# A state-space convolution and a feature-map attention on one core: the written order, read-out engines, PSUM rings, per-unit forms and warm-up products set anew

## The chip, the core and the metric

The kernel runs on one core of one Trainium2 chip. The metric is the device time of one execution in microseconds (us). A core has five engines that matter here: PE (TensorE, with its weight loads shown apart as PEld), DVE (VectorE), ACT (ScalarE), POOL (GpSimd) and SP (the engine whose queue issues most of the DMAs). Each works through its own list of instructions in order; semaphores hold an instruction back until what it reads is there.

## The reference

Two branches of the same input `x` (2048 rows of 512 channels) are mixed by a gate. Branch `a` is a long convolution: a kernel K of 2048 taps per channel is a sum over 128 complex exponentials, and the convolution is done with FFTs. Branch `b` is linear attention of 32 heads of width 16 whose feature map is a softmax of +p and of -p.

```python
g = sigmoid((x * gate_w).sum(-1, keepdims=True))
P = exp(logdA[:, :, None] * l[None, None, :])            # logdA = exp(log_dt) * (A_re + i A_im)
K = einsum("dn,dnl,dn->dl", Cc, P, dB).real
a = irfft(rfft(pad(x)) * rfft(pad(K)))[:2048] + x * Dskip
q, k, v = split_heads(x @ wqkv)
phi = lambda p: concat([softmax(p), softmax(-p)])        # p = q @ w_phi, k @ w_phi
kv, z = einsum(phi_k, v), phi_k.sum(over the rows)
b = (phi_q @ kv / (phi_q @ z + 1e-6)) @ wo
out = g * a + (1 - g) * b
```

## The kernel before, in words

The work is written as 1035 steps (`Plan.add`, `Plan.dma`), each with an engine, a name, what it depends on, and the buffers it takes and frees. They are made in five parts, and nothing in this making sets the order in which they are issued. `Plan.run` reads that order from a table, `ORDER`: two characters are the number of one step. Four more tables are read beside it. `SIDES` gives, for each step that can run on either of two engines (read-outs of PSUM, mostly ACT or DVE), which one. `RINGS` gives, for each step that can take its PSUM tile from either of two rings, which one. `FOURS` (one digit per unit) and `ZPS` (one per pair of key blocks) choose between two forms of a step. `WARM` gives a number to each step that writes a PSUM tile; `heat` (L1561) issues that many products of the identity with a finished table into the fresh tile before the real products, which then overwrite them. In the kernel before, `WARM` is "0".

The stages, by what ACT does, since its list falls into clear parts:

- **Start.** Loads of parameters, `u` (tile `UD`) and weights; sine tables `TB`, `TI`, `TJ` (L284 to L306); folding `w_phi` into the weights (`wtp`, `wps`); `x` transposed (`xps`); then for 16 row blocks keys, `pk` (L704), their exponentials `Ek`, the softmax sums `Zk` (L731, or by products `zk` L725 and L734 where `ZPS` is 1), their reciprocal by a logarithm and an exponential on ACT (`rz`, L741 to L743: `Zk` and the 17th plane of `vr`), values `vp` (L752), and `kn` (L769). In between, the FFT of `u` for each half: `psA` (L586), `psB` (L611), read out to `xst` and written to DRAM as `XUd`.
- **Tables of the exponentials.** `trg` (sines and cosines on ACT), from which DVE makes `Ctab` and `Dtab` (L378).
- **Four phases of four units.** A unit is 32 channels. For each phase ACT first makes eight `cs` tiles (sines, L68, from `args` L1019), then `E` (exponentials, from `args` L1041). DVE makes per unit `A` (L1102, L1107, and L1112 where `FOURS` is 0) and `R` (L1119, L1123); PE multiplies them, `kps` (L178); ACT reads it out to `KD`, PE makes `psA` (L185), ACT reads it to `XA`, and for each quarter of the channels PE makes `psB` (L191), ACT reads it to `XK`, DVE multiplies by `XUX`, PE makes `psz` (L1262), ACT reads it to `Zr`, and it goes through DRAM (`Zd`, `ZT`) to the products `psy` (L1360). The queries' attention (`pq`, `Eq`, `zs`, `den`, `apm`, `ax`, `ops`, `oT`) lies in between.
- **Tail.** The last units in smaller pieces, and the stores to `out` (L1384, L991), issued from SP or ACT.

ACT holds one set of function tables at a time. The steps `tabT` (the set with the sine) and `tabL` (the set with logarithm and exponential) load one by name (L65, `preload_act_table_set`); each is a step of its own, so its place is a place in `ORDER`. A step notes the set it wants (`tab="L"` or `"T"`), but `Plan.run` only asserts that the dependences in `deps` are kept, and `tab` is not one of them. Where an activation stands behind another set, the build puts an `ACT_TABLE_LOAD` ahead of it, with the line of the activation (L68); a logarithm and an exponential get a set each in that case.

## Time and profile before

| | |
|---|---|
| median of 3 runs | 258.6 us (257.18 to 258.92) |
| the profiled execution | 258.5 us; its span, first to last instruction, 256.7 us |
| mean granted TensorE clock | 0.934 |
| DMA | 34.85 MB, 136 GB/s over the span |
| `ACT_TABLE_LOAD` | 10 |

The page gives busy time by engine and, in 40 slices of the span (6.4 us each), the busy share in tenths, the granted TensorE clock and the DMA share. The stretches used below were asked of the trace with ACT's own events as borders: the start of the third table load at 72.15 us (sines for `trg`), the end of the fourth at 103.55, the starts of the fifth, seventh and ninth (127.19, 153.17, 193.31), the end of the read-outs `XA` of units 12 and 13 at 224.60, and the start of 9.9 us at the end in which ACT computes nothing more (246.80).

### The profile page before, as it was taken

Reading aid. Unit: us, or ns where it says so; the run is one execution under the profiler, and the core shown is the slowest. Engines: PE = TensorE matmul, PEld = TensorE weight load, DVE = VectorE, ACT = ScalarE, POOL = GpSimd, SP = SyncE. Lnnn points to the kernel's source line nnn. Section 1 sums busy time; section 2 is a strip of 40 time slices with the busy share of each in tenths; the row PEclk is TensorE's granted clock in tenths of the full one; section 3 lists DMA queues with packets and bytes.
Section 4 is the critical chain, followed back from the end, with each engine's and each line's share of the span. In section 5 each row is a group of like instructions: output and inputs, shape, how many; then the busy total and the mean of one; then the engine's idle time right before and its main releaser. Section 6 shows DMA issues by size and latency. Waiting matters only on the chain.

```text
span 256.7 us, 9697 instructions
## 1 busy us (share of the span) xinstructions
PE 203.7 (79%) x4302; PEld 140.2 (55%) x4322; DVE 232.7 (91%) x315; ACT 221.8 (86%) x307; POOL 7.9 (3%) x21
## 2 busy tenths in 40 slices
PE   0676999999964578898958676899998899896970
PEld 0565665755643424356646533775686566784540
DVE  7699989988799999999999998999999899987781
ACT  3989898999899999989999989999999999863640
POOL 5600000000000000000000000000000000000000
PEclk9999999999997579999999778999999999997995
DMA  6899000336510587300644079215775975991934
GB/s 204 163 219 216 1 3 4 108 111 175 156 33 0 182 241 216 107 4 23 187 128 124 12 212 249 87 44 125 247 167 156 243 194 95 230 336 62 214 72 82
DMA packets 52841, 34.85 MB, mean 136 GB/s; under 512 B 30528, under 2 KB 48320, under 8 KB 52800
## 3 DMA queue, kind: packets, MB, share of 16 engines
q1 hardware_dynamic: 51456, 33.78, 50.5%
q8 instruction: 33, 0.54, 1.0%
q10 hardware_dynamic: 1344, 0.46, 0.9%
q14 instruction: 8, 0.07, 0.1%
HBM read 21.38 MB, written 12.58 MB: 132 GB/s over the span
## 4 chain that ended last, share of the span: by engine, by line
PE 36%; DVE 23%; ACT 23%; DMA 7%; issue 7%; SPq 2%; POOL 0%; ACTq 0%; DVEq 0%; POOLq 0%
PE pk L704 6%; PE vp L752 5%; ACT cs L68 4%; PE kps L178 3%; DMA Zd<-Zr 2%; PE psz L1262 2%; ACT Zr L144 2%; DVE A L1102 2%; DMA ZT<-Zd 2%; ACT L65 2%; DVE R L1119 2%; ACT XA L144 2%; ACT XK L144 2%; DMA ax<-apd 2%; DVE A L1107 2%
## 5 line engine op out<-in xcount | busy, mean ns | idle before, releaser
L68 ACT ACTIVATE cs<-args 128x1024 bf16<-128x1024 f32 x32 | 31.1, 1061 | 0.4 <-PE args L1019 0.4
L178 PE MATMUL kps<-R,A 128*32 128x64 bf16 x1536 | 28.6, 230 | 3.0 <-issue 1.6
L178 PEld LDWEIGHTS <-A 128*32 128x32 bf16 x1536 | 26.5, 160 | 7.5 <-issue 4.4
L1102 DVE TENSOR_TENSOR A<-Ctab,Dtab 128x2048 bf16<-128x2048 bf16 x16 | 19.5, 1217 | 1.3 <-PE kps L178 1.3
L1123 DVE TENSOR_TENSOR R<-E,cs 128x2048 bf16<-128x2048 bf16 x16 | 19.5, 1216 | 0.1
L1107 DVE TENSOR_TENSOR A<-Ctab,Dtab 128x2048 bf16<-128x2048 bf16 x16 | 19.5, 1216 | 0.0
L1119 DVE TENSOR_TENSOR R<-E,cs 128x2048 bf16<-128x2048 bf16 x16 | 19.5, 1216 | 0.0
L144 ACT CAST Zr<-psz 128x1024 bf16<-128x1024 f32 (+1 forms) x17 | 16.5, 990 | 2.2 <-PE psz L1262 0.9
L68 ACT ACTIVATE Ek<-pk 128x512 bf16<-128x512 f32 x32 | 16.7, 600 | 1.8 <-PE pk L704 1.6
L68 ACT ACTIVATE Eq<-pq 128x512 bf16<-128x512 f32 (+1 forms) x28 | 16.7, 686 | 0.6 <-PE pq L838 0.5
L1233 DVE TENSOR_TENSOR t<-XUX,XK 128x2048 bf16<-128x2048 bf16 x14 | 16.9, 1215 | 0.4 <-ACT XK L144 0.4
L68 ACT ACTIVATE E<-args 128x1024 bf16<-128x1024 f32 x16 | 16.7, 1043 | 0.5 <-DVE R L1123 0.5
L611 PE MATMUL psB<-XAu,TB 64*128 64x128 bf16 x256 | 11.8, 250 | 6.6 <-ACT xst L144 3.4
L752 PE MATMUL vp<-WW,xT 128*128 128x512 bf16 x59 | 16.1, 404 | 0.5 <-issue 0.3
L144 ACT CAST XK<-psB 128x1024 bf16<-128x1024 f32 (+1 forms) x17 | 16.4, 992 | 0.0
L144 ACT CAST XA<-psA 128x1024 bf16<-128x1024 f32 (+1 forms) x16 | 15.8, 1017 | 0.6 <-PE psA L185 0.6
L838 PE MATMUL pq<-xT,Wqp 128*128 128x512 bf16 x64 | 15.6, 380 | 0.0
L704 PE MATMUL pk<-WW,xT 128*128 128x512 bf16 x58 | 15.0, 380 | 0.4 <-issue 0.2
L611 PEld LDWEIGHTS <-TB 64*128 64x128 bf16 x256 | 9.7, 111 | 9.9 <-issue 9.8
L1262 PE MATMUL psz<-t,TI 128*128 128x512 bf16 x41 | 13.2, 423 | 1.1 <-ACT XK L144 0.6
L185 PE MATMUL psA<-W,KD 128*64 128x128 bf16 x256 | 9.8, 221 | 4.9 <-ACT cs L68 2.9
L65 ACT ACT_TABLE_LOAD x10 | 12.8, 1283 | 0.9 <-PEq L1615 0.7
(206 smaller groups left out, 496.0 us busy)
## 6 DMA issues: line engine op xcount, KB each, us to landing
XUX<-XUd SPq DMA_DIRECT2D x32, 256.0 KB, 3.7
XUd<-xst SPq DMA_DIRECT2D x8, 512.0 KB, 3.0
ax<-apd SPq DMA_DIRECT2D x16, 256.0 KB, 4.8
Zd<-Zr SPq DMA_DIRECT2D x24, 128.0 KB, 3.1
ZT<-Zd SPq DMA_DIRECT2D x6, 512.0 KB, 5.3
UD<-in_A_u_dram SPq DMA_DIRECT2D x16, 128.0 KB, 4.3
XUd<-xst SPq DMA_DIRECT2D x8, 256.0 KB, 3.9
wqk<-in_B_wqkv_dram SPq DMA_DIRECT2D x1, 1024.0 KB, 5.8
```

Of the source, the lines that this page charges most:

```text
L65: return self.nc.scalar.preload_act_table_set(name)
L68: return self.nc.scalar.activation(**kw)
L144: self.nc.scalar.copy(out=o, in_=i)
L178: nc.tensor.matmul(kps[32 * dj:32 * dj + 32, g4, e, :], lhsT=A[:, ka, :, :, d].rearrange("p a b -> p (a b)"), rhs=R[:, kr, d, :], start=(i ...
L611: nc.tensor.matmul(box.ps[:, c2, sl, :], lhsT=fc.TB[rows, b0:b0 + 2].rearrange("p a b -> p (a b)"), rhs=X.t[rows, k, r0 + sl].rearrange("p ...
L704: nc.tensor.matmul(box.ps[:], lhsT=xT[:, st, kt, :], rhs=g.WW[:, kt, :], start=(kt == 0), stop=(kt == 3))
L752: nc.tensor.matmul(box.ps[:], lhsT=xT[:, st, kt, :], rhs=g.WW[:, 4 + kt, :], start=(kt == 0), stop=(kt == 3))
L1102: nc.vector.tensor_tensor(out=c.A[:, 0:2].rearrange("p o a b c -> p (o a) b c"), in0=g.C[U // 8][:, 0:2, :, d0 % 256:d0 % 256 + 32].rearra ...
L1107: nc.vector.tensor_tensor(out=c.A[:, 2:4].rearrange("p o a b c -> p (o a) b c"), in0=g.C[U // 8][:, 1:3, :, d0 % 256:d0 % 256 + 32].rearra ...
L1119: nc.vector.tensor_tensor(out=c.R[:, :, :, 32:64], in0=t.E[:, 1].unsqueeze(1).to_broadcast([128, 2, 32, 32]), in1=t.cs[:], op=ALU.mult)
L1123: nc.vector.tensor_tensor(out=c.R[:, :, :, 0:32], in0=t.E[:, 0].unsqueeze(1).to_broadcast([128, 2, 32, 32]), in1=t.cs[:, ::-1, :, ::-1], o ...
L1262: nc.tensor.matmul(box.ps[:, hb, :], lhsT=fc.TI[:, k].rearrange("p h a t -> p (h a t)"), rhs=box.t[:, k, 512 * hb:512 * hb + 512], start=( ...
```

## The change

No step, tile, deps entry or shape is changed. The six tables are:

```diff
-    ORDER = ("0405060B0C0D0H0K0d0e0f0y0z0A0L0s0t0u0I0708090J0M0P0g0h0i000S110j0k0l0N0102030T0m0n0o0Q2P0a0b0c0p0q0r0_0W2R100U0O0V120Y2S"
...
+    ORDER = ("0H0I0J0B0C0D2P2R0M0L0K0_000P0Q100d0e0f0y0z0A0p0q0r0s0t0u0708090405060j0k0l0g0h0i0102030a0b0c0m0n0o2v2y2t2x2u0S0U0T0V0W112w2Q"
...
-    SIDES = ("01111101001010101100111011001001100101010000101110000000000001100001100111110100010001100000000000000000000000000000"
-             "0000000000000000000000000000100110000000000000001000010")
-    RINGS = ("001010111111010010100000000000000000000010100000000000001110010000100000001001001010101010100111111110001011000011100001"
-             "1111")
-    WARM = ("0")
-    FOURS = ("0111100101011000")
-    ZPS = ("01000111")
+    SIDES = ("10110101001010101100110111111010010101010010001110000100000010110100101101010100010001100000000000000000000000000000"
+             "0000011000000000000000000011001100000000000000000000010")
+    RINGS = ("00101011111000011010000000000000000000101010000000000000011001000010000000100101001110101010011111101000111100101010"
+             "00010011")
+    WARM = ("00000000600000000060000000005000010000300000000000000030001202000100230210100000000005011060520300000000000000000100"
+             "00000000001000000000003")
+    FOURS = ("0111110101011000")
+    ZPS = ("01000101")
```

What that comes to, step by step: 25 read-outs change their engine, 13 from ACT to DVE and 12 back (`vb` 4 each way, `XAu` 3 and 2, those to `xst` 2 and 1, `bsg` 2 and 1, the copies `UDp` 1 and 2, `bs3` 1 to DVE, `xT` and `XA` 1 each to ACT). `selE` goes from DVE to POOL, `Wphi` from POOL to DVE. Two stores move from SP's queue to ACT's and one from ACT's to SP's. Unit 5 gets the form with four products (no L1112, twice the `kps` products); key pair 6 gets the form without `zk`. Ten steps take their PSUM tile from the other ring. The numbers of `WARM` add up to 67 at 25 places; four of these places, with 15, are `zp` steps whose pair has `ZPS` 0, and these return before the tile is made. The built program has 52 such products at 21 places. It has 30 `ACT_TABLE_LOAD`s, 10 with L65 and 20 with L68.

The first place is ACT's list where `trg` begins. Before:

```order
L68 ACTIVATE Zk<-Zk 128x128
L68 ACTIVATE vr<-Zk 128x4x32
L65 ACT_TABLE_LOAD
L68 ACTIVATE trg<-pb_267 128x1024
L68 ACTIVATE trg<-pb_266 128x1024
L144 CAST XAu<-psA 128x256x4 x2
L68 ACTIVATE trg<-pb_266 128x1024
L402 ACTIVATE pb_267<-pb_266 128x1024
```

and now:

```order
L65 ACT_TABLE_LOAD
L68 ACTIVATE trg<-pb_297 128x1024
L68 ACT_TABLE_LOAD
L68 ACTIVATE Zk<-Zk 128x128
L68 ACT_TABLE_LOAD
L68 ACTIVATE vr<-Zk 128x4x32
L68 ACT_TABLE_LOAD
L68 ACTIVATE trg<-pb_298 128x1024
L144 CAST vb<-vp 128x512
L144 CAST XAu<-psA 128x256x4
```

The seventh reciprocal of the softmax sums (`Zk`, `vr`) now stands between two sine steps; the eighth does too, further down the list, with three loads of its own.

The second place is ACT's list at the first phase's `cs` tiles. Before:

```order
L144 CAST xst<-psB 128x2x4x4x32 x2
L68 ACTIVATE cs<-args 128x1024 x8
L65 ACT_TABLE_LOAD
L68 ACTIVATE E<-args 128x1024
L68 ACTIVATE Eq<-pq 128x4x128 x4
L68 ACTIVATE E<-args 128x1024
L68 ACTIVATE Eq<-pq 128x4x128 x8
```

and now:

```order
L144 CAST xst<-psB 128x2x4x4x32 x2
L68 ACT_TABLE_LOAD
L68 ACTIVATE E<-args 128x1024
L68 ACT_TABLE_LOAD
L68 ACTIVATE cs<-args 128x1024 x2
L68 ACT_TABLE_LOAD
L68 ACTIVATE Eq<-pq 128x4x128 x2
L68 ACT_TABLE_LOAD
L68 ACTIVATE cs<-args 128x1024 x6
L68 ACT_TABLE_LOAD
L68 ACTIVATE E<-args 128x1024
L68 ACTIVATE Eq<-pq 128x4x128 x2
```

One `E` and one pair of `Eq` have moved in ahead of and between the `cs` tiles; the `tabL` step itself (L65) comes nine activations behind the last row.

The third place is the end of ACT's list. Before:

```order
L144 CAST Zr<-psz 128x512 x2
L144 CAST Zr<-psz 128x1024
L991 DMA out_dram<-xT 32x4x384 x2
L1384 DMA out_dram<-xT 512x1x128 x2
```

and now:

```order
L1384 DMA out_dram<-xT 32x12x256 x2
L144 CAST xT<-bps 128x2x128
L144 CAST Zr<-psz 128x512 x2
L144 CAST Zr<-psz 128x1024
L65 ACT_TABLE_LOAD
L1384 DMA out_dram<-xT 512x1x128 x2
L1384 DMA out_dram<-xT 32x12x256 x2
```

Four stores of other quarters came to ACT and the two of L991 left it; two of the four now stand behind the store of the last quarter.

By the stretches named above, the table loads stand like this (from ACT's two lists; a stretch of the change is the one with the same activations):

| stretch of before, us | loads before | loads now |
|---|---|---|
| 0 to 72.15 | 2 | 2 |
| 72.15 to 103.55 | 2 | 12 |
| 103.55 to 127.19 | 0 | 1 |
| 127.19 to 153.17 | 2 | 7 |
| 153.17 to 193.31 | 2 | 5 |
| 193.31 to 224.60 | 2 | 2 |
| after 224.60 | 0 | 1 |

33 lines of the change are left out of this document (16 added, 17 removed).

## The prediction

> **What bounds the kernel now.** I read the page's busy times first, then a table of stretches cut at ACT's own events, then ACT's rows at a table load.
>
> ```profile
> PE 203.7 (79%) x4302; PEld 140.2 (55%) x4322; DVE 232.7 (91%) x315; ACT 221.8 (86%) x307; POOL 7.9 (3%) x21
> ...
> PE 36%; DVE 23%; ACT 23%; DMA 7%; issue 7%; SPq 2%; POOL 0%; ACTq 0%; DVEq 0%; POOLq 0%
> ```
>
> No engine owns the chain (the second row): it changes hands. The shares are means, so the stretches decide. Columns: from and to, length, then busy us of PE, PEld, DVE, ACT, POOL, then the granted clock, the DMA share and GB/s.
>
> ```profile
> 0.00:72.15 72.15, 57.90 (x911) 40.24 (x921) 62.55 (x110) 62.18 (x105) 7.91 (x21) 1.00 0.50 122
> 72.15:103.55 31.40, 20.60 (x307) 12.54 (x309) 30.26 (x51) 30.79 (x32) 0.00 (x0) 0.78 0.47 139
> 103.55:127.19 23.64, 20.84 (x515) 12.40 (x513) 23.43 (x35) 22.02 (x40) 0.00 (x0) 1.00 0.26 74
> 127.19:153.17 25.98, 18.81 (x462) 12.73 (x463) 25.91 (x29) 24.97 (x31) 0.00 (x0) 0.87 0.43 118
> 153.17:193.31 40.14, 36.25 (x841) 26.58 (x843) 39.19 (x42) 39.37 (x49) 0.00 (x0) 0.96 0.58 152
> 193.31:224.60 31.29, 27.78 (x686) 20.88 (x684) 30.38 (x30) 29.26 (x31) 0.00 (x0) 1.00 0.78 186
> 224.60:246.80 22.20, 19.55 (x465) 13.44 (x464) 17.62 (x21) 13.19 (x21) 0.00 (x0) 0.92 0.65 186
> 246.80:256.70 9.90, 1.92 (x132) 1.35 (x130) 3.38 (x4) 0.00 (x0) 0.00 (x0) 0.68 0.42 82
> ```
>
> From 72.15 to 224.60, 152.45 us, DVE is busy 149.2 and ACT 146.4 (sums of five rows). Two engines are full at once: work taken off one alone gains little, but work put on ACT has only 152.45 - 146.41 = 6.0 us of idle time to go into. I call this stretch the middle. PE is busy 124.3 of it. Before and behind the middle all engines have gaps.
>
> **The table loads.** The change turns ACT's 10 table loads into 30. What one takes:
>
> ```profile
> L65 ACT ACT_TABLE_LOAD x10 | 12.8, 1283 | 0.9 <-PEq L1615 0.7
> ```
> ```profile
> 71.83 0.31 ACT L68 ACTIVATE vr<-Zk 128x128 bf16<-128x128 f32 x1
> 72.15 1.28 ACT L65 ACT_TABLE_LOAD   x1
> 73.44 2.01 ACT L68 ACTIVATE trg<-pb 128x1024 bf16<-128x1024 f32 x2
> 75.36 1.00 ACT L144 CAST XAu<-psA 128x1024 bf16<-128x1024 f32 x1
> ```
>
> The load waits for nothing and starts 0.01 us behind the activation (71.83 + 0.31 = 72.14), the next one 0.01 behind the load. Two ordinary instructions overlap: the pair ends at 75.45 and the cast starts at 75.36, 0.09 earlier. An inserted load therefore costs 1.28 + 0.01 + 0.09 = 1.38 us of ACT's time. Twelve loads instead of 2 stand in the stretch from 72.15 on, 1 instead of 0, 7 instead of 2 and 5 instead of 2 in the next three, 2 and 2 in the fifth: 10 + 1 + 5 + 3 = 19 more in the middle, 19 x 1.38 = **26.2 us**. The twentieth stands behind ACT's last read-out:
>
> ```profile
> 245.77 1.03 ACT L144 CAST Zr<-psz 128x1024 bf16<-128x1024 f32 x1
> 250.49 0.69 DVE L1373 TENSOR_TENSOR xT<-psy,gT 128x512 bf16<-128x512 f32 x1 [0.97 <-PE psy L1360]
> 251.21 1.66 ACTq L1384 DMA_DIRECT2D out_dram<-xT  x2
> ```
>
> What follows it on ACT is the last store, and that waits for DVE's product, 4.4 us after the read-out (246.80 to 251.18): the load lies in that gap and costs nothing; without the gap, 1.28.
>
> The middle's other work on ACT grows too. Two reciprocals that before ended at 72.14 are now between sine steps, four activations by the rows:
>
> ```profile
> L68 ACT ACTIVATE Zk<-Zk 128x128 f32<-128x128 f32 x8 | 2.6, 326 | 0.7 <-DVE Zk L734 0.7
> L68 ACT ACTIVATE vr<-Zk 128x128 bf16<-128x128 f32 x8 | 2.5, 311 | 0.3
> L144 ACT CAST vb<-vp 128x512 bf16<-128x512 f32 x7 | 4.2, 595 | 1.2 <-PE vp L752 0.8 <-DVE vr L761 0.4
> ```
>
> 2 x (0.326 + 0.311) = 1.3 us; two `vb` read-outs come to ACT there (1.2), and an `xst` read-out left it (about 1.0, as the cast at 75.36): **+1.5 us**. So ACT's work in the middle is at least 146.4 + 26.2 + 1.5 = 174.1 us, DVE's 149.2 and a little: ACT alone sets the middle. Of ACT's 6.0 us idle some vanishes, because DVE and PE, which it waited for, now run ahead; but ACT's order was not drawn around these loads, and an `E` or `XK` that comes late holds DVE, whose answer ACT needs a few rows on. Bounds: none left (174.1) and twice as much (186.1). I take half, 3.0, nearer the low end since 96% of ACT's middle is already work (146.4 of 152.45): 177.1, against 152.45, **+24.7 us**.
>
> The Trainium skill (ScalarE: Activation LUTs, What ACT_TABLE_LOAD costs) gives a switch of sets as about 1283 ns of load and a drain of about 1380 ns, 2.66 us together. The load is the row's number; of the drain the rows at 72.15 show nothing. By it, 19 x 2.66 = 50.5 us, an estimate, would come on top, about 308 us.
>
> **The dummy products.** 52 are in the program. A stream of the same shape, warm and at a low clock:
>
> ```profile
> 33.02 1.89 PE L704 MATMUL pk<-WW,xT 128*128 128x512 bf16 x8
> 94.89 1.46 PE L752 MATMUL vp<-WW,xT 128*128 128x512 bf16 x3
> ```
> ```profile
> L704 PE MATMUL pk<-WW,xT 128*128 128x512 bf16 x58 | 15.0, 380 | 0.4 <-issue 0.2
> ```
>
> One takes 0.380, so the seven others in 1.89 us follow at 0.216 each; three in 1.46 are at most 0.49 each. So the 52 are 11 us of PE (52 x 0.216), at most 25. Nearly all stand in the middle, where PE has 152.45 - 124.28 = 28 us free now and some 25 more when ACT stretches it. What they could gain is a higher clock where it falls to 0.78 and 0.87; there ACT is busy 98% and 96%, PE waits for it, and faster products end no wait. Bounds: a gain of 1 us, and a loss of 3 where six of them stand ahead of a `psB` that ACT waits for (6 x 0.49 = 2.9). I take 0. The cover is the table loads themselves; without them PE's 28 us must do.
>
> **Per-unit forms and engines.**
>
> ```profile
> L1112 DVE TENSOR_TENSOR A<-A 128x2048 bf16<-128x2048 bf16 x8 | 9.8, 1219 | 0.1
> L731 DVE TENSOR_REDUCE Zk<-Ek 128x64 f32<-128x1024 bf16 x8 | 9.3, 1208 | 0.0
> L734 DVE TENSOR_REDUCE Zk<-zk 128x128 f32<-128x512 f32 x4 | 2.8, 692 | 1.4 <-PE zk L725 1.3
> ```
>
> Unit 5 loses one sum (-1.22), key pair 6 gets two long reductions for a short one (2 x 1.21 - 0.69 = +1.73), and the moved read-outs nearly cancel (13 against 12): DVE has about 1 us more. It is hidden by ACT's 25; if ACT were not late, it would cost its 1 us. The other PSUM rings and the products of unit 5 in place of `zk` likewise lie in PE's free time.
>
> **Start and tail.** At the start PE waits for the first weights, which now are first on SP's queue, 0.47 us sooner:
>
> ```profile
> 7.09 1.89 PE L525 MATMUL wtp<-ident,wqk 128*128 128x128 bf16 x16 [7.09 <-DMA wqk<-in_B_wqkv_dram]
> 1.20 0.42 SPq L1507 DMA_DIRECT2D wqk<-in_B_wqkv_dram  x1
> 0.73 0.40 SPq L211 DMA_DIRECT2D Bim<-in_A_B_im_dram  x1
> 8.42 1.05 POOL L468 TENSOR_TENSOR Wphi<-wc,mask 128x512 bf16<-128x512 bf16 x1 [4.50 <-DMA wc<-in_B_w_phi_dram]
> ```
>
> But `Wphi` is now on DVE ahead of the read-out of those products, and waits for a DMA that lands at 8.42; behind it `wT` and all that PE does next are queued. These two about cancel. ACT gets to its first sine step without the two reciprocals and without the last sums: 1.3 us less work in a stretch in which it is idle 10.0 us, so between 0 and 2: **-1.0**. At the end ACT issues four stores where it issued two (1.66), the added two by
>
> ```profile
> 251.21 1.34 SPq L1384 DMA_DIRECT2D out_dram<-xT  x2
> ```
>
> 1.34 us later than the last store before: +1.3. DVE, no longer the last to be late, may give back some of the 9.1 us from the end of the last `E` to the end of that unit's last sum:
>
> ```profile
> 221.71 1.05 ACT L68 ACTIVATE E<-args 128x1024 bf16<-128x1024 f32 x1
> 230.59 1.22 DVE L1112 TENSOR_TENSOR A<-A 128x2048 bf16<-128x2048 bf16 x1
> ```
>
> Of it six instructions of DVE, about 7 us, are that unit's own. Bounds -3 and +2 for the tail as a whole, I take **+1.0**.
>
> **The sum**, against the profiled execution's 258.5 us (span 256.7 and 1.8 around it; the median of the runs, 258.6, is the same within 0.1): 258.5 + 24.7 - 1.0 + 1.0 = 283.2, say **283 us**, slower by 9.5%. With the low ends (174.1 in the middle, -2, -1, -3) 274.2, with the high ends (186.1, +3, 0, +2) 297.2; high ends together are unlikely.
>
> **The rivals.**
>
> - *The loads go into idle time.* ACT's table loads wait for nothing, so they can run while ACT would wait for PE or DVE. For: a load needs no operand. Against: only 6.0 us idle in the middle. Were all of that used and the start and the tail 3 us and 5 us shorter through the new order, 258.5 + 21.7 - 8 = about 272. Below 273: 0.10.
> - *The order opens more waits than the loads.* With PE idle while ACT reloads, the clock falls to half over more of the middle, and the dummy products stand in front of real ones at that clock. For: the clock was 0.78 where PE was busy 20.60 of 31.40. Against: 96% of ACT's middle was work. Every term at its high end, 297. Above 293: 0.10.
> - *Each load drains the engine first.* The mechanism would be a wait of one long activation, some 1.04 us (E in the page's groups is below), at each of 19 loads: 283 + 20 = 303. Against: 0.01 us ahead of the load at 72.15. 0.02. The Trainium skill's rule above (ScalarE: Activation LUTs, What ACT_TABLE_LOAD costs) is of this kind.
>
> ```profile
> L68 ACT ACTIVATE E<-args 128x1024 bf16<-128x1024 f32 x16 | 16.7, 1043 | 0.5 <-DVE R L1123 0.5
> ```
>
> - *The loads do not run, the other side.* If the 20 loads of line 68 were merged away before they reach the chip, 20 x 1.38 leave the list and the order alone is left: 258.5 + 1.5 - 1.0 + 1.0 - 3 = 257, not slower. It decides from about 18 loads taken away. Against: the list of before has 10 loads and the trace shows x10. 0.03; within that I give faster by over 1% a third.
>
> **How the numbers follow.** Forecast 0.75, rivals 0.10, 0.10, 0.02 and 0.03. Range 273 to 293: it leaves out 0.1 below, with the other side, and 0.1 above. A measurement of this kernel can tell about 1% from no change: faster 0.01, same 0.02, slower 0.97.
>
> **What would show it.** In the profile of the change: 30 table loads of 1.28 us; ACT busy about 248 us and above DVE's 234; from the first load behind the last `Ek` to the read-outs `XA` of units 12 and 13 about 177 us, with the growth in the stretches of 10, 5 and 3 added loads (about 14, 7 and 4 us) and little in the last; DVE with 25 us more idle there, released by ACT; the low-clock slices gone or not, without a difference. Wrong: fewer loads, or loads shorter than 1.28; ACT idle over 12 us in the middle; or the last stretch shorter than before by as much as the first grew.

## The result: 296.7 us, and the profile after

The changed kernel takes 296.72 us (median of four executions, 295.31 to 297.21) against 258.02 us of the kernel before, timed beside it: 1.149 times as long, 95% interval 1.143 to 1.155. Timed a second time it took 294.74 us, 1.148 times the kernel before (1.141 to 1.156). Ratios and their intervals are taken over executions at the chip's usual speed and medians over all (one execution of run f3 below took 626.6 us), so a ratio is not always the quotient of two medians. The change is slower, as forecast, but by 38.7 us and not by 24.7, and 3.7 us beyond the range. The profiled execution took 297.17 us with a span of 295.3.

The page of the changed kernel, first its busy times, then rows of its picture in 40 slices (one digit is the busy share of a slice in tenths; PEclk is the granted clock):

```profile
PE 224.6 (76%) x4430; PEld 149.2 (51%) x4430; DVE 234.3 (79%) x316; ACT 248.2 (84%) x326; POOL 9.5 (3%) x21
...
DVE  7999999898476991799884597698997998865490
ACT  4998799989979999999969998999996997324750
...
PEclk9999999999667575999959999999997997966997
...
L68 ACT ACT_TABLE_LOAD x20 | 25.7, 1283 | 0.3
```

ACT's busy time rose from 221.8 to 248.2 us, as forecast (248), and is now above DVE's. The 20 loads of line 68 ran, each 1283 ns. DVE has holes from the eleventh slice on (4, 1 and 4 tenths at the deepest in the middle), where before no slice from the third to the last but one fell below 7. At the place where the first added loads stand, ACT's timeline (start, length, what) reads:

```profile
70.20 1.06 ACT L68 ACTIVATE trg<-pb 128x1024 bf16<-128x1024 int16 x1
71.28 1.28 ACT L68 ACT_TABLE_LOAD   x1
72.57 0.31 ACT L68 ACTIVATE Zk<-Zk 128x128 f32<-128x128 f32 x1
72.90 1.28 ACT L68 ACT_TABLE_LOAD   x1
74.19 0.31 ACT L68 ACTIVATE vr<-Zk 128x128 bf16<-128x128 f32 x1
74.51 1.28 ACT L68 ACT_TABLE_LOAD   x1
```

A load starts 0.01 to 0.02 us behind the activation ahead of it, and the activation behind it starts 0.01 us after its end. Between the two sine steps two activations of 0.31 us drag three loads of 1.28 with them. The gap of 0.01 us is the answer to the rule of the Trainium skill (ScalarE: Activation LUTs, What ACT_TABLE_LOAD costs) of a drain of about 1380 ns at a switch: the trace does not show it, ahead of the load or behind.

The table of stretches, cut at the same events on ACT as the prediction's (from and to, length, busy us of PE, PEld, DVE, ACT, POOL, granted clock, DMA share, GB/s; the seventh border is here the end of ACT's last read-out):

```profile
0.00:68.90 68.90, 57.47 (x908) 39.43 (x909) 63.97 (x110) 60.73 (x100) 9.46 (x21) 1.00 0.55 132
68.90:118.58 49.68, 30.11 (x332) 15.35 (x331) 33.45 (x54) 47.33 (x50) 0.00 (x0) 0.69 0.30 88
118.58:140.21 21.63, 19.35 (x510) 12.23 (x509) 20.37 (x30) 21.00 (x37) 0.00 (x0) 1.00 0.35 105
140.21:173.09 32.88, 24.02 (x538) 15.39 (x539) 23.12 (x27) 30.10 (x36) 0.00 (x0) 0.90 0.18 47
173.09:220.38 47.29, 39.81 (x868) 28.25 (x866) 41.72 (x44) 45.33 (x53) 0.00 (x0) 1.00 0.50 130
220.38:264.53 44.15, 31.89 (x757) 23.56 (x756) 36.74 (x35) 30.11 (x33) 0.00 (x0) 0.87 0.75 198
264.53:284.37 19.84, 19.25 (x379) 13.15 (x379) 11.53 (x16) 12.29 (x19) 0.00 (x0) 0.85 0.32 70
284.37:295.30 10.93, 2.72 (x166) 1.78 (x152) 3.38 (x4) 1.28 (x2) 0.00 (x0) 0.80 0.57 119
```

Against the rows of before: the start is 3.25 us shorter; the second and third stretch together, with 11 added loads, 16.3 longer (71.31 against 55.04); the fourth, with 5, 6.9; the fifth, with 3, 7.15; the sixth, **with none, 12.9** (44.15 against 31.29); what is behind it 1.3 shorter (30.77 against 32.10).

The middle (second to sixth row) is now 195.63 us and ACT works 173.87 of them, where the prediction had 177.1 and 174.1. ACT's work was forecast to 0.2 us. Its idle time was taken as 3.0 us, at most 12, and is 21.8: 14.0 in the sixth stretch (44.15 - 30.11), 7.7 in the other four.

Who keeps ACT waiting in the middle (line, tile, releaser: us in total, times, longest):

```profile
ACT Ctab L144 <- DVE xT L1370: 10.1, 2, 7.3
ACT XA L144 <- PE psA L185: 3.3, 3, 2.5
ACT Zr L144 <- PE psz L1262: 1.9, 2, 1.2
ACT xst L144 <- PE psB L611: 1.9, 1, 1.9
```

The first row is two of the three read-outs of step `Y` (line 144 copies `psy` into `Ctab`). Each follows a product `ou` of DVE (line 1370) that reads the same `psy`. ACT's and DVE's timelines at the longer of the two waits:

```profile
254.68 1.02 ACT L144 CAST XA<-psA 128x1024 bf16<-128x1024 f32 x1
263.03 0.59 ACT L144 CAST Ctab<-psy 128x512 bf16<-128x512 f32 x1 [7.33 <-DVE xT L1370]
263.51 1.02 ACT L144 CAST XA<-psA 128x1024 bf16<-128x1024 f32 x1
```
```profile
254.58 0.68 DVE L1049 TENSOR_TENSOR E<-E,Gtab 128x1024 bf16<-128x1024 bf16 x1
255.18 1.22 DVE L1119 TENSOR_TENSOR R<-E,cs 128x2048 bf16<-128x2048 bf16 x1
257.76 1.22 DVE L1102 TENSOR_TENSOR A<-Ctab,Dtab 128x2048 bf16<-128x2048 bf16 x1 [1.36 <-PE kps L178]
258.91 1.22 DVE L1107 TENSOR_TENSOR A<-Ctab,Dtab 128x2048 bf16<-128x2048 bf16 x1
260.04 1.22 DVE L1123 TENSOR_TENSOR R<-E,cs 128x2048 bf16<-128x2048 bf16 x1
261.18 1.22 DVE L1112 TENSOR_TENSOR A<-A 128x2048 bf16<-128x2048 bf16 x1
262.31 0.68 DVE L1370 TENSOR_TENSOR xT<-psy,gT 128x512 bf16<-128x512 f32 x1
```

The last row is the `ou` in question. In the change it stands behind six products for a later unit, 7.7 us; before, it stood ahead of the first of them. DVE's timeline of before there:

```profile
223.88 0.68 DVE L1370 TENSOR_TENSOR xT<-psy,gT 128x512 bf16<-128x512 f32 x1
224.49 0.68 DVE L1049 TENSOR_TENSOR E<-E,Gtab 128x1024 bf16<-128x1024 bf16 x1
```

On ACT the read-out now stands ahead of the `XA` of unit 13, for which the chain of products goes on; before, it stood behind that `XA`.

The shorter wait, 2.80 us, has another cause. Its `ou` waited itself, for PE:

```profile
225.69 0.69 DVE L1370 TENSOR_TENSOR xT<-psy,gT 128x512 bf16<-128x512 f32 x1 [0.66 <-PE psy L1360]
```

PE made that `psy` late, behind a stall of 1.57 us that the last section shows.

The second and the fourth row of the waits are mostly the dummies' doing: without dummies, in run e2 below, they are 0.8 and 0.2 us. From the chain that ended last, the pieces of line 1563 (the dummy products) that lie on it in the middle:

```profile
80.41 2.72 PE psB L1563 x6
...
151.06 2.29 PE psA L1563 x5
...
180.00 1.24 PE psB L1563 x5
...
182.84 0.81 PE psA L1563 x3
```

7.1 us of dummy products stand on the chain, each time ahead of a product whose read-out ACT waits for.

### The profile page after: what moved, and what is told of

The parts are those of the page before. It is cut to its first block, busy times and chain, and to the rows that moved or that the text cites. A ratio compares the mean times of both kernels' runs of the same rounds, so it can differ in the third digit from the quotient of the medians.

```text
span 295.3 us, 9937 instructions
## 1 busy us (share of the span) xinstructions
PE 224.6 (76%) x4430; PEld 149.2 (51%) x4430; DVE 234.3 (79%) x316; ACT 248.2 (84%) x326; POOL 9.5 (3%) x21
## 3 DMA queue, kind: packets, MB, share of 16 engines
q10 hardware_dynamic: 2656, 1.05, 1.7%
## 4 chain that ended last, share of the span: by engine, by line
ACT 42%; PE 31%; DVE 15%; issue 7%; DMA 2%; SPq 0%; POOL 0%; ACTq 0%; DVEq 0%; POOLq 0%
ACT L68 8%; ACT cs L68 6%; PE pk L704 4%; PE vp L752 4%; ACT XA L144 3%; ACT L65 3%; ACT Eq L68 2%; ACT trg L68 2%; DMA ZT<-Zd 2%; PE psy L819 2%; ACT E L68 2%; ACT xst L144 2%; PE psB L611 2%; PE psA L586 2%; DVE A L1102 2%
## 5 line engine op out<-in xcount | busy, mean ns | idle before, releaser
L68 ACT ACTIVATE cs<-args 128x1024 bf16<-128x1024 f32 x32 | 31.1, 1055 | 0.1
L178 PEld LDWEIGHTS <-A 128*32 128x32 bf16 x1600 | 27.3, 160 | 6.2 <-issue 2.9
L68 ACT ACT_TABLE_LOAD x20 | 25.7, 1283 | 0.3
L1102 DVE TENSOR_TENSOR A<-Ctab,Dtab 128x2048 bf16<-128x2048 bf16 x16 | 19.5, 1219 | 6.1 <-PE kps L178 6.1
L1119 DVE TENSOR_TENSOR R<-E,cs 128x2048 bf16<-128x2048 bf16 x16 | 19.5, 1218 | 1.2 <-PE kps L178 1.1
L144 ACT CAST XA<-psA 128x1024 bf16<-128x1024 f32 (+1 forms) x17 | 16.3, 981 | 4.8 <-PE psA L185 4.8
L1123 DVE TENSOR_TENSOR R<-E,cs 128x2048 bf16<-128x2048 bf16 x16 | 19.5, 1216 | 0.0
L1107 DVE TENSOR_TENSOR A<-Ctab,Dtab 128x2048 bf16<-128x2048 bf16 x16 | 19.5, 1216 | 0.0
L838 PE MATMUL pq<-xT,Wqp 128*128 128x512 bf16 x64 | 18.5, 425 | 0.7 <-ACT Eq L68 0.6
L144 ACT CAST Zr<-psz 128x1024 bf16<-128x1024 f32 (+1 forms) x17 | 16.3, 986 | 2.7 <-PE psz L1262 1.9
L68 ACT ACTIVATE Ek<-pk 128x512 bf16<-128x512 f32 x32 | 16.8, 600 | 1.7 <-PE pk L704 1.6
L1049 DVE TENSOR_TENSOR E<-E,Gtab 128x1024 bf16<-128x1024 bf16 x16 | 10.9, 684 | 9.0 <-ACT E L68 9.0
L68 ACT ACTIVATE E<-args 128x1024 bf16<-128x1024 f32 x16 | 16.6, 1040 | 0.4 <-DVE R L1123 0.4
L191 PE MATMUL psB<-XA,TB 128*128 128x128 bf16 (+2 forms) x192 | 11.2, 209 | 7.6 <-ACT XA L144 7.1
L68 ACT ACTIVATE Eq<-pq 128x512 bf16<-128x512 f32 (+1 forms) x28 | 16.7, 686 | 0.3 <-PE pq L838 0.2
L191 PEld LDWEIGHTS <-TB 128*128 128x128 bf16 x192 | 9.8, 102 | 12.2 <-DVE xT L1370 5.5
L1019 PE MATMUL args<-selE,statC 64*128 64x512 bf16 x32 | 7.3, 450 | 10.8 <-ACT cs L68 9.2
```

Of the source, the lines that this page charges most:

```text
L68: return self.nc.scalar.activation(**kw)
L144: self.nc.scalar.copy(out=o, in_=i)
L178: nc.tensor.matmul(kps[32 * dj:32 * dj + 32, g4, e, :], lhsT=A[:, ka, :, :, d].rearrange("p a b -> p (a b)"), rhs=R[:, kr, d, :], start=(i ...
L191: nc.tensor.matmul(ps[:, sl, :], lhsT=fc.TB[:, 3 * (r0 + sl) + 1:3 * (r0 + sl) + 3].rearrange("p a b -> p (a b)"), rhs=XA[:, r0 + sl], sta ...
L838: nc.tensor.matmul(box.ps[:, m - m0, :] if late else box.ps[:], lhsT=g.Wqp[:, kt, 128 * m:128 * m + 128], rhs=xT[:, 4 * b:4 * b + 4, kt, : ...
L1102: nc.vector.tensor_tensor(out=c.A[:, 0:2].rearrange("p o a b c -> p (o a) b c"), in0=g.C[U // 8][:, 0:2, :, d0 % 256:d0 % 256 + 32].rearra ...
```

## The experiments

All timed kernels in one table. A ratio is to the kernel before, timed on the same chip at the same time, since the kernel before itself took 255.8 to 258.1 us from one occasion to another; differences of 1% between rows of different groups are not told apart by the medians, so the stretches of the profiled executions, one for each kernel, stand beside them. The start of kernels that begin alike is 68.9 in some of these and 70.3 in others, so a difference of 1 to 2 us between two stretches may be chance. "Start" ends at the table load ahead of the first `trg`, "middle" at the second `XA` of units 12 and 13, "behind" is the rest of the span.

| kernel | us | ratio, 95% interval | start | middle | behind |
|---|---|---|---|---|---|
| before | 258.0 | 1 | 72.15 | 152.44 | 32.11 |
| the change | 296.7 | 1.149 (1.143 to 1.155) | 68.90 | 195.63 | 30.77 |
| e1 ten loads | 269.3 | 1.044 (1.038 to 1.049) | 68.91 | 166.45 | 30.14 |
| e2 no dummies | 292.7 | 1.126 (1.117 to 1.135) | 70.58 | 189.94 | 29.48 |
| e3 before, 19 loads | 282.2 | 1.093 (1.088 to 1.098) | 72.38 | 177.06 | 30.96 |
| e4 before, dummies | 261.5 | 1.016 (1.011 to 1.021) | 72.23 | 155.79 | 31.08 |
| e5 `Y` later | 291.2 | 1.136 (1.131 to 1.140) | 68.92 | 187.12 | 33.26 |
| e6 ten loads, no dummies | 263.8 | 1.029 (1.024 to 1.033) | 68.95 | 163.76 | 29.09 |
| e7 the same, `Y` later | 260.1 | 1.016 (1.010 to 1.022) | 68.89 | 158.47 | 33.04 |
| e8 grouped by table | 278.0 | 1.084 (1.079 to 1.090) | 80.86 | 164.16 | 32.38 |
| e9 33 dummies | 291.4 | 1.145 (1.138 to 1.152) | 68.92 | 188.82 | 30.16 |
| e10 `ou` earlier | 292.1 | 1.147 (1.142 to 1.152) | 70.31 | 190.58 | 29.81 |
| e11 before, start of the change | 256.5 | 1.005 (1.001 to 1.009) | 73.84 | 151.88 | 30.48 |
| e12 last stretch as before | 290.5 | 1.141 (1.135 to 1.146) | 68.91 | 190.34 | 29.15 |
| f1 the change again | 294.7 | 1.148 (1.141 to 1.156) | 70.25 | 194.93 | 30.42 |
| f2 no dummies, `Y` later, `ou` earlier | 290.0 | 1.129 (1.122 to 1.137) | 68.92 | 186.85 | 32.63 |
| f3 before, 19 loads and dummies | 288.0 | 1.122 (1.116 to 1.127) | 72.21 | 184.49 | 30.60 |
| f4 e12 without dummies | 287.3 | 1.121 (1.115 to 1.127) | 68.92 | 188.39 | 30.49 |
| f5 f4 with before's engines | 287.8 | 1.120 (1.112 to 1.127) | 70.25 | 187.26 | 30.29 |
| f6 f5 with before's rings | 285.1 | 1.104 (1.095 to 1.114) | 68.93 | 182.17 | 32.30 |

Theory A: the loads, the dummies and the read-outs behind `ou` are causes of their own. Theory B: the loads make all else late, and without them the order costs nothing.

### The loads

**e3: the loads alone, in the order of before.**

```diff
+    AGAIN = (75, 76, 77, 78, 79, 80, 82, 83, 84, 85, 104, 127, 129, 137, 138, 139, 144, 146, 153)
+    n = 0
     def __call__(self, **kw):
+        self.n += 1
+        if self.n in self.AGAIN:
+            self.nc.scalar.preload_act_table_set(self.set)
         return self.nc.scalar.activation(**kw)
```

> The kernel before with 19 table loads more, each of the table that is loaded already (so the values stay the same), 10 ahead of the sines of the first middle stretch, 1, 5 and 3 in the next three, as the change has them. Theory A: the loads alone cost 258.0 + 26 = 284 less the part that falls into ACT's 6 us of idle time: 278 to 285. Theory B: loads that stand in the list make other engines late in turn, which costs again: 290 to 297.

282.2 us, 24.1 more than before. The stretches of this kernel from the start to the second `XA` of units 12 and 13:

```profile
72.38:141.43 69.05, 44.67 (x822) 25.41 (x821) 54.59 (x84) 67.65 (x83) 0.00 (x0) 0.78 0.31 88
141.43:175.26 33.83, 19.73 (x463) 13.06 (x463) 26.79 (x30) 31.95 (x37) 0.00 (x0) 0.85 0.34 90
175.26:219.78 44.52, 37.77 (x848) 27.26 (x848) 39.88 (x42) 43.61 (x51) 0.00 (x0) 0.92 0.53 138
219.78:249.44 29.66, 27.22 (x676) 20.75 (x677) 29.31 (x28) 29.11 (x31) 0.00 (x0) 1.00 0.77 192
```

The middle is 177.06 us long, where the prediction's sum for the changed kernel had 177.1, and ACT is idle 4.7 of it (177.06 - 172.32). The three stretches with 11, 5 and 3 loads grew by 14.0, 7.9 and 4.4 us, 26.2 together, against 19 x 1.38 = 26.2; the last one, with none, is 1.6 shorter than before. So the price of a load was right, and ACT's idle time is inside its bounds, for these loads **in the order of before**. That the two lengths agree to 0.1 us is partly chance: e3 lacks the 1.5 us of other work that the prediction's sum holds, and has 1.7 us more idle time than the 3.0 taken. What the changed kernel takes beyond this comes from its other parts.

**e1: the change with ten loads.**

```diff
     def begin(self, name):
+        self.set = name
         return self.nc.scalar.preload_act_table_set(name)
     def __call__(self, **kw):
+        if self.set != (TRIG if kw["func"] == ACT.Sin else LN_EXP):
+            kw["func"] = ACT.Square
+            kw.pop("bias", None)
```

> The changed kernel with 10 table loads in place of 30; an activation that stands in the wrong table's stretch computes a square, so those exponentials, logarithms and sines are left out. Theory A (three separate causes that add up: 19 loads on the path at about 1.38 us, read-outs Y that wait for DVE's late ou, dummy products ahead of needed ones): 296.7 - 26.2 = about 270, 266 to 273, with ACT still idle for some 15 us or more in the middle. Theory B (all of the growth follows from the loads, which make everything behind them late; the order alone costs nothing): 257 to 261, with ACT's idle time in the middle back near 6 us.

269.3 us, 27.4 below the change, and the middle is still 14.0 us longer than before (166.45 against 152.44) although ACT's work in it is the same (146.97 against 146.41). Theory B is out: without one load more than before, ACT idles 19.5 us there. The sixth stretch alone is 42.45 us long in this run, 11.2 more than before, so most of its growth in the change needs no added load.

**e8: the same ten loads with the whole computation.** The steps follow the change's order, but an activation waits in the list until its table's turn as before groups them; dummies and late read-outs are taken away as in e7.

```diff
-    WARM = ("00000000600000000060000000005000010000300000000000000030001202000100230210100000000005011060520300000000000000000100"
...
+    WARM = ("0")
```

In the list of steps the sine table of step 121 comes 37 places later, the table of step 538 25 places sooner and that of step 892 117 sooner.

> The whole computation in the changed kernel's order, but each table's activations held back until their table is loaded as the kernel before groups them, so that 10 loads do; 26 or so steps move by over ten places; no dummies, the two read-outs Y later. Theory A: the causes of the growth are gone: 254 to 262. Theory B: 258 to 264, since the order as such brings nothing.

Missed: 278.0 us, above what both theories gave. ACT's timeline at the second sine table:

```profile
80.19 0.32 ACT L68 ACTIVATE Zk<-Zk 128x128 f32<-128x128 f32 x1
80.54 0.31 ACT L68 ACTIVATE vr<-Zk 128x128 bf16<-128x128 f32 x1
80.86 1.28 ACT L65 ACT_TABLE_LOAD   x1
```

The table waits for the last reciprocal, so the start alone takes 80.86 us, and the middle 164.16, 5.7 more than in e7. In the change's order the operands of the two tables' activations come interleaved, at least here. Grouped in this one way, the order costs waits of 18 us (278.0 against 260.1 of e7) in place of the 27 of the loads; other groupings were not tried.

### The dummies

**e2: the change without them; e4: before with them.**

```diff
-    WARM = ("00000000600000000060000000005000010000300000000000000030001202000100230210100000000005011060520300000000000000000100"
...
+    WARM = ("0")
```

(e4 puts the change's WARM into the kernel before, in the other direction.)

> The changed kernel without its 52 dummy products. Theory A: the four groups of dummies on the chain of after (2.7, 2.3, 1.2 and 0.8 us) go and nothing else fills the gap: 296.7 - 6 = about 291, 289 to 293. Theory B: the dummies only fill time in which PE waits for ACT anyway: 296.7, within 1.5. If the dummies keep the clock up to any use: above 298.

> The kernel before with the dummy products of the change, by the same table of places (52 run). Theory A: there is the same PE time ahead of read-outs that ACT waits for: 258 + 2 to 6 = 260 to 264. Theory B: PE has room under ACT: 258, within 1.5.

292.7 us, 2 to 4 below the change's two medians and 5.7 less in the middle; 261.5 us, 3.5 above before and 3.35 more in the middle. Theory A both times. They cost with or without added loads, so the table loads do not cover them.

**e9: without 19 of the 52**, the four groups that the chain showed.

```diff
             n.warm = int(next(warm, 0)) if n.name in self.HOT and n.ring in ("ps", "bk", "pf") else 0
+            if n.i in (263, 586, 624, 674):
+                n.warm = 0
```

> The changed kernel without 19 of its 52 dummy products: the four groups of 6, 5, 5 and 3 that stand ahead of a product that ACT waits for, and lay on its chain of waits. The other 33 stay. If a dummy costs by its place: the same as without any, about 4 us below the change, 291 to 294. If it costs by the product: 19/52 of 4, about 1.5 us, 294.5 to 296.

291.4 us, by the median as expected of a cost by place: within 1.3 us of the kernel without any, and the middle is 6.8 us shorter than the change's, e2's 5.7. The ratios speak the other way: 1.145 is nearer the change's 1.149 than e2's 1.126. The kernel before took 255.8 us at the one time and 258.0 at the other. The stretches speak for the place: the 33 dummies that are left cost nothing that can be seen in the middle. For the whole time that is not settled.

**f3: loads and dummies together, in the order of before.** The edits of e3 and e4 in one kernel.

> The kernel before with the 19 loads more and the 52 dummies, in its own order. If the two add: 256.5 + 24 + 3.5 = 284 (282 to 286). If PE's time under a waiting ACT hides the dummies: 280 to 281.

288.0 us; the two do not just add. 24.1 and 3.5 are 27.6, the run shows 29.9, and the middle grew by 7.4 us over e3, where the same 52 products cost 3.35 without the loads. PE's timelines of e4 and then of f3 at the same five dummies show a part of the reason:

```profile
136.16 1.24 PE L1564 MATMUL psA<-TB,ident 128*128 128x512 bf16 x5 [1.20 <-ACT cs L68]
```
```profile
153.65 2.29 PE L1571 MATMUL psA<-TB,ident 128*128 128x512 bf16 x5 [1.19 <-ACT cs L75]
```

The five took 1.24 us in one and 2.29 in the other, as in the change. In f3 and in the change the dummies of this group ran at nearly half the pace of e4. That is 1.05 us of the 4.1 by which 7.4 exceeds 3.35; where the rest comes from is open. Where ACT reloads, PE has less to do (busy 30.11 of 49.68 us in the change's second stretch) and the granted clock is lower there, 0.69 against 0.78 before. That the one follows from the other was not tried apart.

### The last stretch

**e5: two of the read-outs `Y` later on ACT**, behind `XA` of their unit and behind `XK` of unit 13. ACT's list at the second of them, change and edit:

```diff
 L144 CAST oT_4794<-ops 128x1024
-L144 CAST XA<-psA 128x32x32
-L144 CAST Ctab_75<-psy 128x4x128
-L144 CAST XA<-psA 128x32x32
+L144 CAST XA<-psA 128x32x32 x2
 L144 CAST KD<-kps 128x512
```

> The changed kernel with two of the three read-outs Y written later on ACT: the first behind the XA of the same unit, the second behind XA, KD and XK of units 12 and 13, so that ACT's wait for DVE's ou no longer holds these back. Nothing else is moved. Theory A: the waits of 2.8 and 7.3 us ahead of these read-outs go, most of the last stretch's growth of 12.9 us with them: 296.7 - 7 to 11 = 286 to 290. Theory B: what stands behind them is late for other reasons and waits just as long elsewhere: 295 to 298.

291.2 us, 3.6 to 5.5 below the change's two medians, in part what theory A wanted. The sixth stretch fell by 8.2 us (44.15 to 35.97), but what lies behind grew from 30.77 to 33.26. A third of it came back. The total lies between the two theories, nearer to A.

**e10: the `ou` earlier on DVE**, the other end of the same wait.

```diff
 L1119 TENSOR_TENSOR R<-E,cs 128x64x32
+L1370 TENSOR_TENSOR xT<-psy,gT 128x4x128
 L1102 TENSOR_TENSOR A<-Ctab_76,Dtab 128x2048
 L1107 TENSOR_TENSOR A<-Ctab_76,Dtab 128x2048
 L1123 TENSOR_TENSOR R<-E,cs 128x64x32
 L1112 TENSOR_TENSOR A<-A 128x2048
-L1370 TENSOR_TENSOR xT<-psy,gT 128x4x128
```

> The changed kernel with one product of DVE written earlier: the ou of the second Y, which stood behind A and R of unit 15, is put ahead of them, where the kernel before had it; ACT's list stays. If the 7.3 us wait is that one product's place: 296.7 - 5 to 8 = 289 to 292, with the wait ahead of the second Y under 2 us. If DVE's list is what runs late there and the place does not matter: 295.5 to 298.

The `ou` is now ahead of the last four of the six products, while before it was ahead of all six. 292.1 us. The wait ahead of the second `Y` fell from 7.33 to 1.81 us, and the sixth stretch from 44.15 to 38.15. By the ratio, 1.147 against 1.149, nothing is gained; by the medians 2.6 to 4.6. The place of that one product made the wait; how much of it the whole kernel gains stays within what the two occasions differ.

**e6 and e7: no loads, no dummies, and then `Y` later.** The edits of e1 and e2; of e1, e2 and e5. Misplaced activations compute a square again.

> The changed kernel with 10 table loads (misplaced activations compute a square, so their own values are left out) and no dummy products. Theory A: 296.7 - 26.2 - 6 = about 264, 261 to 267. Theory B: 257 to 261, no further from the run with ten loads and dummies than 1.5.

> The changed kernel with 10 table loads (misplaced activations compute a square, so their own values are left out), no dummy products, and the two read-outs Y written later: what is left of the change is its order, engines of read-outs and forms. Theory A: 296.7 - 26.2 - 6 - 7 to 11 = 253 to 258. Theory B: as without the later read-outs, within 1.5.

263.8 and 260.1 us, as theory A had them (264, and 253 to 258, by 2 us missed). With the three causes gone the changed kernel is 1.6% above before (1.0 to 2.2%), not below: what is left of the change has no gain of its own that would show. In e6 the 7.30 us wait ahead of the second `Y` is still there, so it is not the added loads that make it.

**e12 and f4: the last 225 steps in the order of before**, with and without dummies. The edit replaces the table `ORDER`; written as the rule that makes the new one it is:

```diff
         order = [64 * code[a] + code[b] for a, b in zip(self.ORDER[0::2], self.ORDER[1::2])]
+        head = order[:810]
+        order = head + [i for i in ORDER_OF_BEFORE if i not in head]
```

> The changed kernel with its last 225 steps (from the fifth change to the sine table on) in the order of the kernel before; loads, dummies and forms stay. If the order alone made the last stretch 12.9 us longer: 296.7 - 10 to 13 = 284 to 287. If it is long because the steps ahead of it come late: 294 to 298.

> The changed kernel with its last 225 steps in the order of before, and no dummies. If the causes add: the change minus 6 (order of the last stretch) minus 5 (dummies) = about 285, 283 to 288; if the last stretch's order was the larger part: 280 to 283.

290.5 us, 4 to 6 below the change's two medians and between the two forecasts; and 287.3, 7.4 below f1, which was timed beside it, inside the range for causes that add. The order alone does not make the last stretch long: the sixth stretch is still 39.2 us long in e12 and 38.8 in f4, with the order of before in it, where before has 31.3.

**f1 and f2: the change again, and the change without the located causes but with its loads.**

> The changed kernel as it is, timed on the chip that times the next three, so that their differences need no second chip: 1.149 of before, 294 to 298. Both theories.

> The changed kernel without dummies, with both read-outs Y later and the ou of the second one earlier; loads and all other order stay. If the causes add: the change minus 5 (dummies) minus 4 to 8 (last stretch) = 284 to 288. If dummies and late read-outs fill the same wait: 289 to 292.

294.7 and 290.0 us. Taking dummies, late `Y` and late `ou` away together brings 4.7 us, where 9 or more were expected of a sum. By the ratios, 1.129 against e2's 1.126, that is no more than the dummies alone. The sixth stretch is 36.7 us long (31.3 before), and behind it stand 32.63 us in place of 30.42. Once the dummies are gone, moving these single steps brings nothing more that would show.

**f5 and f6: then the engines, then the rings of the last part.**

```diff
+    AT = {758: 'SP', 761: 'SP', 919: 'ACT', 920: 'ACT', 921: 'DVE', 924: 'ACT', 926: 'ACT', 1015: 'DVE'}
+    RING = {816: 'ps', 818: 'pf', 840: 'ps', 916: 'pf', 963: 'ps', 976: 'ps', 989: 'pf', 1013: 'pf', 1016: 'pf'}
...
+            n.at, n.ring = self.AT.get(n.i, n.at), self.RING.get(n.i, n.ring)
```

(f5 has `RING` empty. The eight entries of `AT` are five read-outs and three stores, not four and four. The change gives 14 steps another ring than before, not ten; the nine of `RING` are those of the last part.)

> The changed kernel without dummies, its last 225 steps in the order of before and there on the engines of before too (4 read-outs, 4 stores). If the engines were the rest: the part from the last sine table on falls from 69.3 to 61-64 us, 280 to 283 in all. If not: 287, within 1.5.

> The same, with the PSUM rings of before for the 9 products of that part as well. If the rings were the rest (a product of KD, XA or Zr that waits for the read-out of another in its ring): 61 to 64 us for that part, 280 to 283 in all. If neither: 287, and the rest lies in how the part is entered.

287.8 and 285.1 us. The sixth stretch of f4, of f5 and of f6:

```profile
218.50:257.31 38.81, 30.23 (x670) 22.95 (x670) 31.64 (x30) 29.78 (x32) 0.00 (x0) 0.87 0.73 181
```
```profile
220.41:257.51 37.10, 29.01 (x670) 21.66 (x670) 31.70 (x30) 29.85 (x32) 0.00 (x0) 0.91 0.73 185
```
```profile
219.12:251.10 31.98, 27.72 (x678) 20.85 (x678) 29.24 (x27) 29.26 (x31) 0.00 (x0) 1.00 0.80 194
```

f5 is where it was expected if the engines were not the rest. f6 falls between its two forecasts: 285.1 us in all, and 64.3 us for the part behind the last sine table. In the sixth stretch the engines brought 1.7 us and the rings 5.1: with the nine products back in their old PSUM rings it is 31.98 us long, before's 31.3 within 0.7, with the clock at 1.00 again. Behind it 2 us come back (32.30 against 30.29), so that the two medians differ by 2.7 us, and the two intervals of the ratio overlap a little.

One of the nine is a product `ops` (step 916). PE's timeline at it in f5, then in f6:

```profile
251.78 1.03 PE L930 MATMUL ops<-Eq,KVbd 128*128 128x256 bf16 x8 [1.88 <-ACT KD L145]
```
```profile
245.52 1.05 PE L930 MATMUL ops<-Eq,KVbd 128*128 128x256 bf16 x8
```

`ops` does not read `KD`. So its wait in f5 is taken to be for the PSUM tile that this read-out of ACT frees; in f6 it has no wait. PE's stalls (last section) do not make the difference: they are 2.9 us of f5's sixth stretch and 2.5 of f6's.

So the rings of the change are enough to keep the last stretch long, with the order and engines of before. The change's order with the rings of before was not run, so what the order does alone stays open.

### The start

**e11: the first 317 steps of the change in the kernel before**, with their engines and rings.

> The kernel before with the first 317 steps in the order, on the engines and in the rings of the change, the rest as before: no more loads, no dummies. If the shorter start (68.9 against 72.2 us) is a gain of its own: 258.0 - 3.2 = about 255, 253.5 to 256.5. If it only shifts work across the border into the next stretch: 257 to 259.

256.5 us against 255.8 (ratio 1.005, 1.001 to 1.009): no gain. The start of its profiled execution is 73.84 us and not 68.9, so the shorter start is not in the order of these steps alone, and this run cannot say whether a shorter one would be a gain. A part of it is work moved across the border: in before ACT spends 2.0 us on the last two reciprocals and the waits ahead of them, from the end of its last `XAu` (70.16) to the load (72.15). The change has these reciprocals behind the load, e11 ahead of it again. No version here beats the kernel before.

## Why the prediction was wrong

**Right: the sign, the loads and ACT's work.** 30 loads of 1283 ns, no gap around them, ACT busy 248.2 us, its work in the middle 173.87 us against 174.1. e3 measured the loads by themselves: 24.6 us more in the middle and 24.1 in all, for a forecast of 24.7 in the middle.

**The step that failed** is "I take half, 3.0" with its upper bound "twice as much", that is, the idle time of ACT in the middle as a share of what it was before, and with it "little in the last" stretch. ACT idles 21.8 us, 18.8 more than was taken and well over the 12 that the prediction gave as a sign of being wrong. The bound came from the loads: more work on ACT leaves it less to wait for. That holds, 4.7 us in e3, for the order of before. But the change replaced that order, and where products stand on DVE and PE that ACT needs, it waits for them however much it has to do elsewhere. The prediction read the new lists for loads and not for what a read-out of ACT now stands behind: the later `ou`, 7.3 us of waits in the sixth stretch, could be seen in DVE's list. The earlier one, 2.8 us, could not, since it waited for PE.

**The last stretch.** Of its 12.9 us, DVE has 6.4 us more work to do ahead of its end (36.74 against 30.38; 35 products for 30) and 6.5 us more idle (7.4 against 0.9). DVE set this stretch already before, busy 30.38 of 31.29 us. The runs fit these two halves. With before's order in it (f4), DVE's work there is 31.64 us and the idle time still 7.2. With before's engines (f5) the idle time is 5.4, and with before's rings too (f6) 2.7, at 29.24 us of work. So the work of later units that is written ahead of what units 12 and 13 need lengthens the stretch by about its own length, and most of the idle time comes with the engines and the rings. That the added work itself is the cause of the first half is read from the rows: f4 changes the whole order of the part and not only that work. What is left for the part behind is less (11.53 against 17.62 in the seventh row), but PE sets that one, busy 19.25 of 19.84 us, and 2.4 us is all that it gave back. The rivals had the order only through PE's clock; DVE was not named, and the prediction put the other PSUM rings into PE's free time.

**The dummies** were taken as 0, with a loss of up to 3 us "where six of them stand ahead of a `psB` that ACT waits for". Such a group is on the chain with 2.72 us, three more groups are, and in the middle the 52 cost 3.35 us in the order of before and 5.7 to 7.4 beside the loads. "The cover is the table loads themselves" was wrong: a load holds ACT and makes PE wait, but the dummies wait too. The rows of e4 and f3 show PE idle for 1.2 us, until ACT has made a `cs`, and the dummies begin only then: they stand behind the idle time and not in it.

**The loads in the other order** cost 27.4 us by e1, against 24.1 in e3.

**The small terms.** The start was 3.25 us shorter in the profiled execution (-1.0 forecast, bounds 0 and -2), 1.9 in f1's; the part behind the middle 1.3 shorter (+1.0 forecast, bounds -3 and +2). The middle is 18.5 us longer than forecast, and the start and the part behind together 4.6 shorter, so the total misses by less than the middle does; that is luck. The twentieth load shows in the last row, ACT busy 1.28, and lies in the gap it was given. DVE's 1 us more is 1.6 (234.3 against 232.7); whether it hides was not tried apart.

**The rivals.** "The order opens more waits than the loads" is nearest to what happened, with "every term at its high end, 297" close to 296.7, but not by its mechanism alone: of what stands beyond the loads' cost the dummies are some 3 to 7 us by the runs above, and most of the rest lies in the last stretch, in the order and the rings. "Each load drains the engine first" is out: no gap at any of the rows above, 1.27 us per load in e3 (24.1 us for 19), which loads the same table again, and 1.37 in e1 (27.4 us for 20), which takes away the change's real switches. "The loads go into idle time" and "the loads do not run" are out with e1 and e3.

**The account.** f6 has the change's loads but the twentieth and its order up to the last part, and there the order, engines and rings of before, without dummies: 27.7 us above the kernel before that was timed beside it (257.3). These are the loads, 24 to 27, and a little. To e2, with the last part as changed, it is 7.6 us more (292.7 - 285.1; 5.5 by the ratios), and to the change with its dummies 2 to 4 (5.9 by the ratios): 27.7 + 7.6 + 2 to 4 is 37.3 to 39.3, where 38.7 was measured. The steps of this sum are differences in a row, so that it comes out is no test of it. How the 7.6 divide into order, engines and rings is not settled.

## What to carry to other kernels

When a list is written anew, count what each engine's work is, but also read, for each read-out or store on the bounding engine, which instruction of another engine releases it and what now stands ahead of that one; a price per added instruction is right only in the order in which it was measured. Work of later units placed ahead of earlier ones can be free on an engine with room; in the stretch that this engine sets, it cost about its own length here. Read the PSUM ring of a product like an operand: it can hold the product back until another product is read out. A dummy product ahead of one that is waited for waits as long as that one does, so it is paid for most of its length; five of them took 1.24 us in one kernel and 2.29 in another.

## What the runs showed that was not expected

- A load of the table that is loaded already takes as long as a change. The rows of e3, the 19 added loads and the ten of the program:

```profile
L74 ACT ACT_TABLE_LOAD x19 | 24.4, 1283 | 0.3
L66 ACT ACT_TABLE_LOAD x10 | 12.8, 1283 | 0.9 <-PEq L1622 0.7
```

- PE stalls for 1 to 2 us in the middle of a run of like products, with no releaser in the profile. From PE's timelines of the change and of f4:

```profile
222.63 0.22 PE L819 MATMUL psy<-wo,oT 128*128 128x128 bf16 x1 [1.57 <-issue]
```
```profile
222.93 0.23 PE L1359 MATMUL psy<-ZT,TF 64*32 64x128 bf16 x3 [2.20 <-issue]
226.66 0.27 PE L177 MATMUL kps<-R,A 128*32 128x64 bf16 x3 [1.28 <-issue]
```

  Each of the 20 profiles has one to three such stalls of over 0.9 us, all later than 190 us; in f4's sixth stretch they come to 3.5 us. In the change and the kernels made from it at least one falls within 10 us of the last sine table; in before they stand at 233 and 250 us, behind the last stretch. What makes them was not tried.
